# A long convolution and two expert layers on one core: the filter stage and the first two convolution chunks reordered

## The chip, the cores and the metric

The kernel runs on one core of a Trainium2 chip. The metric is device time in microseconds (us) of one execution; each kernel is run several times and the median counts. A profile is one execution, recorded apart from the timed runs.

## The reference, cut to what matters

```python
h_filt = (np.maximum(pos_emb @ w1, 0.0) @ w2) * np.exp(-0.01 * pos)[:, None]
u = x * v                                     # (2, 12480, 128)
y = irfft(rfft(u, 2 * S, axis=1) * rfft(h_filt, 2 * S, axis=0)[None], axis=1)[:, :S]
a = (x * y).reshape(24960, 128)
h = a @ moe_w_in;  b = where(h > 0, h, exp(min(h, 0)) - 1) @ moe_w_out     # 128 -> 2048 -> 128
h = b @ moe2_w_in; out = (h * cos(h)) @ moe2_w_out
```

A filter is made from position embeddings by two small matrix products, a long causal convolution is done through a Fourier transform, and two expert layers follow.

## The kernel before, in words

The program has three stages, each engine follows the written order of its own instructions (the schedule is written by hand), and TensorE (PE) runs through all of them.

**Filter** (lines 203 to 307). 16 chunks `c`. `rank(c)` (L257) is one product of the embeddings with `w1`; `relu(c)` (L262) takes it on ScalarE (ACT) to `r`, and GpSimd (POOL) splits `r` into a rounded part `r_h` and a rest `r_l`; `taps(c, half)` (L271) are 12 products a chunk with `w2`, and `window` (L280) scales them into `h_all` on VectorE (DVE) with one of eight columns left to ACT. `taps` follow `rank` three chunks behind. Products with a constant tile (`warm_up`, L216) fill PE before that.

**Convolution** (lines 310 to 477). 32 chunks of four channels, each with three sequences `k`: 0 and 1 are the two batches, 2 is the filter. For each, `st_a` (first transform, DVE's `za` and `zb`, POOL's `z_t`), `st_b` (second transform; for the filter ACT copies its result to `hr` and `hi_f`, for a batch DVE multiplies by them: `ya`, `ps_b`, `y_t`, and ACT rounds to `yh`), `lo_y` (POOL's rest `yl`), `st_c` (back transform, `wa`, `wb`, `w_t`) and `st_d` (last product, `at`, written to DRAM). `prod` (L318) makes `u_t` on POOL. A list `steps` (L465) gives one pass `p` its order; a step of the list works on chunk `p`, `p-1` or `p-2`. `ps_a`, `ps_b` and `ps_c` have one PSUM buffer each.

Between the steps the 64-bit weights of the expert layers are decoded, 32 jobs in two halves. `top` takes `Decode.bits` (L123) one piece further: piece 1 is `ps_w` and `sq` on ACT, piece 2 DVE's `size` and ACT's `keep`, piece 3 DVE's second `ps_w` and ACT's `power`, piece 4 DVE's `mag` and ACT's `lf`, then DVE's `pw` and piece 1 of the next job. `low` takes `Decode.parts` (L152) one piece further: POOL's product on `lf`; POOL's `full` (which reads `mag`) and ACT's `hi`; POOL's `lo` and the stores. A pass holds four `top` and three `low`. The tiles `mag`, `lf` and `pw` have two buffers, so those of job `j` take the place of those of job `j-2`.

**Expert layers** (lines 480 to 658), which the change doesn't touch.

```python
steps = ((st_b, 1, 0), (prod, 0, 1), (top, 0, 0), (lo_y, 1, 0), (low, 0, 0), (top, 0, 1), (st_a, 0, 2),
         (st_c, 2, 1), (top, 0, 2), (lo_z, 0, 2), (low, 0, 1), (st_b, 1, 1), (st_a, 0, 0), (lo_y, 1, 1),
         (st_d, 2, 0), (low, 0, 2), (st_c, 1, 0), (prod, -1, 0), (st_b, 0, 2), (st_a, 0, 1), (top, 0, 3),
         (st_d, 2, 1))
```

Of the kernel before, what the change touches and what calls it, by code (L numbers as in the profile page):

```python
# [9 lines left out]
F32 = mybir.dt.float32  # L10
# [3 lines left out]
AF = mybir.ActivationFunctionType  # L14
# [6 lines left out]
NB = 128  # L21
# [59 lines left out]
def hyena_moe_kernel(ctx: ExitStack, tc: tile.TileContext, x, v, pe, w1, w2,  # L81
# [92 lines left out]
    with tc.manual_schedule():  # L174
        nc.vector.memset(below, BELOW)
        with ExitStack() as cs:
# [26 lines left out]
            with ExitStack() as fs:  # L203
# [5 lines left out]
                ph = fs.enter_context(tc.tile_pool(name="ph", bufs=4, space=PSUM))  # L209
                NP = 4  # L210
                NCK = NB // 2 // NP
                NW = 3
                warm = f1.tile([128, 512], F32, name="warm")
                nc.vector.memset(warm, 0.5)

                def warm_up(n):  # L216
                    w_ps = pw.tile([128, 512], F32, name="w_ps")
                    nc.tensor.matmul(w_ps[:, 0:n], warm[:, 0:128], warm[:, 0:n], start=True, stop=True)  # L218

                w1_t = f1.tile([2 * FO, 2 * FO], F32, name="w1_t")  # L220
                w2_t = f1.tile([2 * FO, 2 * D], F32, name="w2_t")
                w2_h = f1.tile([2 * FO, 2 * D], F32R, name="w2_h")
# [6 lines left out]
                        nc.sync.dma_start(pes[c], pe[:, c * NP * NA:(c + 1) * NP * NA])  # L229

                load_pe(0)
                nc.vector.memset(w1_t, 0.0)
                nc.vector.memset(w2_t, 0.0)
                for k in range(2):
                    nc.scalar.dma_start(w1_t[k * FO:(k + 1) * FO, k * FO:(k + 1) * FO], w1)
                    nc.scalar.dma_start(w2_t[k * FO:(k + 1) * FO, k * D:(k + 1) * D], w2)
                nc.scalar.dma_start(win_t[:, :, 0], win)
                for c in range(1, 4):
                    load_pe(c)
                for _ in range(4):  # L240
                    warm_up(512)

                def load_tables():
                    nc.scalar.dma_start(fa_t, fa)
                    nc.scalar.dma_start(tw_t, tw)
                    nc.scalar.dma_start(ti_t, ti)
                    nc.scalar.dma_start(g_t, g)
                    nc.scalar.dma_start(dft_t, dft)

                def split_tables():  # L250
                    copy_r(dft_h, dft_t)
                    nc.vector.tensor_tensor(dft_l, dft_t, dft_h.bitcast(F32), op=ALU.subtract)

                copy_r(w2_h, w2_t)
                nc.vector.tensor_tensor(w2_l, w2_t, w2_h.bitcast(F32), op=ALU.subtract)
# [23 lines left out]

                def window(c, half):  # L280
                    ps, b = hp_.pop((c, half)), (2 * c + half) * NP
                    n = NP if half else NW
                    sl = slice(b, b + n)
                    nc.vector.tensor_tensor(h_all[:, :, sl].rearrange("a d b -> a b d"), ps[:, 0:n],
                                            win_t[:, sl].to_broadcast([NA, n, D]), op=ALU.mult)
                    for k in range(n, NP):
                        nc.scalar.activation(h_all[:, :, b + k], ps[:, k], AF.Copy, scale=win_t[:, b + k])

                for c in range(NCK + 4):
                    if c < NCK:  # L290
                        rank(c)
                        relu(c)
                    if 0 <= c - 3 < NCK:
                        taps(c - 3, 0)
                        taps(c - 3, 1)
                        window(c - 3, 0)
                        window(c - 3, 1)
                    if c < 3:
                        warm_up(512)
                        warm_up(512)  # L300
                    if c == 2:
                        load_tables()
                    if c == NCK - 2:
                        load(0)
                        load(1)
                    if c == NCK - 1:
                        split_tables()


            with ExitStack() as vs:  # L310
                p1 = vs.enter_context(tc.tile_pool(name="p1", bufs=1))
                p2 = vs.enter_context(tc.tile_pool(name="p2", bufs=2))
                pa = vs.enter_context(tc.tile_pool(name="pa", bufs=1, space=PSUM))
                pd = vs.enter_context(tc.tile_pool(name="pd", bufs=1, space=PSUM))
                bank = vs.enter_context(tc.tile_pool(name="bank", bufs=1, space=PSUM))
                us, zz, yy, hh, ww = {}, {}, {}, {}, {}

                def prod(c, k):  # L318
                    if c < NCH:
# [12 lines left out]
                    nc.gpsimd.tensor_tensor(yl, y, yh.bitcast(F32), op=ALU.subtract)  # L332
                    yy[c, k] = (yh, yl)

                def st_a(c, k):
                    ps = pa.tile([NB, 2, 512], F32, name="ps_a")
                    for s in range(DC):
                        lhs = h_all[:, c * DC + s] if k == 2 else us[c, k][:, s]
                        o = (s % 2) * 2 * NF
                        nc.tensor.matmul(ps[:, s // 2, o:o + 2 * NF], lhs, fa_t, start=True, stop=True)  # L340
                    n = 4 * NF
                    t1 = p2.tile([NB, 2 * n], F32, name="za")
                    t2 = p2.tile([NB, 2 * n], F32, name="zb")
                    for q, t in ((0, t1), (1, t2)):
                        nc.vector.tensor_tensor(bank2(t), ps[:, :, 0:n],  # L345
                                                tw_t[:, q:q + 1].to_broadcast([NB, 2, n]), op=ALU.mult)
                    z = p2.tile([NB, 2, DC * NF], F32, name="z_t")
                    nc.gpsimd.tensor_tensor(z.rearrange("p r (s k) -> p r s k", s=DC),  # L348
                                            parts(t1, NF), parts(t2, NF)[:, ::-1], op=ALU.add)
# [10 lines left out]
                    zz[c, k] = (zh, zl)  # L360

                def st_b(c, k):
                    ps = pa.tile([NB, 2, 512], F32, name="ps_b")
                    n = DC * NF
                    mS, C, Sn = (slice(q * NB, (q + 1) * NB) for q in range(3))
                    prs = (((C, 0), (Sn, 1)), ((C, 1), (mS, 0)))
                    z = zz.pop((c, k))
                    for r in range(2):
                        for j, (sl, q) in enumerate(prs[r]):
                            if k == 2:  # L370
                                zh, zl = z
                                mm = ((dft_h, zh), (dft_l, zh), (dft_h, zl))
                            else:
                                mm = ((dft_t, z),)
                            for i, (a, b) in enumerate(mm):
                                nc.tensor.matmul(ps[:, r, 0:n], a[:, sl], b[:, q], start=j == 0 and i == 0,  # L376
                                                 stop=j == 1 and i == len(mm) - 1)
# [19 lines left out]
                def st_c(c, k):  # L397
                    yh, yl = yy.pop((c, k))
                    last = c == NCH - 1
                    ps = pa.tile([NF, 2, 512], F32, name="ps_c", tag="ps_a" if last and k else "ps_c")  # L400
# [59 lines left out]
                def top(c, k):  # L460
                    next(bits, None)

                next(bits)
                prod(0, 0)
                steps = ((st_b, 1, 0), (prod, 0, 1), (top, 0, 0), (lo_y, 1, 0), (low, 0, 0), (top, 0, 1), (st_a, 0, 2),  # L465
                         (st_c, 2, 1), (top, 0, 2), (lo_z, 0, 2), (low, 0, 1), (st_b, 1, 1), (st_a, 0, 0), (lo_y, 1, 1),
                         (st_d, 2, 0), (low, 0, 2), (st_c, 1, 0), (prod, -1, 0), (st_b, 0, 2), (st_a, 0, 1), (top, 0, 3),
                         (st_d, 2, 1))
                for p in range(NCH + 2):
                    for f, back, k in steps:  # L470
                        if 0 <= p - back < NCH or f in (top, low):
                            f(p - back, k)
                    load(p + 2)
                for _ in bits:
                    pass
# [221 lines left out]
```

## Time and profile before

| | us |
|---|---|
| median of 3 runs (2925.21 to 2925.38) | 2925.26 |
| span of the profiled execution | 2922.3 |
| first taps of the filter | 17.30 |
| first `st_d` of the convolution | 90.06 |
| first product of the expert layers | 694.41 |

The span runs from the first to the last instruction; what lies around it is 3.0 us against the median of the runs. PE is busy 99% of the span, DVE 85%, ACT 73%, POOL 90%. [...] A timeline row that merges several instructions gives the start of the first and the time they cover.

### The profile page before, as it was taken

Reading aid. Unit: us, or ns where it says so; the run is one execution under the profiler, and the core shown is the slowest. Engines: PE = TensorE matmul, PEld = TensorE weight load, DVE = VectorE, ACT = ScalarE, POOL = GpSimd, SP = SyncE. Lnnn points to the kernel's source line nnn. Section 1 sums busy time; section 2 is a strip of 40 time slices with the busy share of each in tenths; the row PEclk is TensorE's granted clock in tenths of the full one; section 3 lists DMA queues with packets and bytes.
Section 4 is the critical chain, followed back from the end, with each engine's and each line's share of the span. In section 5 each row is a group of like instructions: output and inputs, shape, how many; then the busy total and the mean of one; then the engine's idle time right before and its main releaser. Section 6 shows DMA issues by size and latency. Waiting matters only on the chain.

```text
span 2922.3 us, 40341 instructions
## 1 busy us (share of the span) xinstructions
PE 2888.7 (99%) x13580; PEld 2393.3 (82%) x13580; DVE 2497.0 (85%) x3241; ACT 2146.6 (73%) x3332; POOL 2632.8 (90%) x1908
## 2 busy tenths in 40 slices
PE   8999999998999999999999999999999999999999
PEld 6878787886888888888888887888888888888887
DVE  5888888887998998899899998888888888888887
ACT  3322323224988898888888888888888888888887
POOL 4888888886999999999999998999999999999998
PEclk9999999998999999999999999999999999999999
DMA  3333333333000000000000001000000000000000
GB/s 105 90 81 88 97 89 86 88 83 97 14 11 14 11 12 14 14 11 11 14 11 14 11 11 60 11 14 11 14 11 14 11 11 14 11 14 11 13 12 14
DMA packets 83104, 96.82 MB, mean 33 GB/s; under 512 B 6106, under 2 KB 68088, under 8 KB 82898
## 3 DMA queue, kind: packets, MB, share of 16 engines
q1 hardware_dynamic: 77072, 88.20, 10.6%
q10 hardware_dynamic: 5826, 6.04, 0.7%
q8 instruction: 109, 1.79, 0.3%
q14 instruction: 97, 0.79, 0.1%
HBM read 59.94 MB, written 34.28 MB: 32 GB/s over the span
## 4 chain that ended last, share of the span: by engine, by line
PE 92%; ACT 3%; DVE 2%; issue 2%; POOL 1%; DMA 0%; ACTq 0%; POOLq 0%; DVEq 0%
PE h_ps L545 35%; PE o_ps L614 34%; PE ps_b L376 8%; PE ps_c L408 6%; PE ps_a L340 4%; PE ps_d L426 4%; ACT e L582 1%; DVE e L575 1%; DVE e L584 1%; ACT e L573 1%; PE h_ps L277 1%; ACT gh L97 1%; ACT ot L622 1%; PE w_ps L218 0%; PE r_ps L259 0%
## 5 line engine op out<-in xcount | busy, mean ns | idle before, releaser
L106 POOL TENSOR_TENSOR gl<-e,gh 128x960 fp32r<-128x960 f32 x780 | 1463.7, 1888 | 88.6 <-ACT gh L97 45.3
L545 PE MATMUL h_ps<-xh,w 128*128 128x480 f32 x3328 | 1022.3, 388 | 15.5 <-DVE e L562 5.5
L614 PE MATMUL o_ps<-gh,w 128*128 128x480 f32 x3120 | 933.0, 380 | 0.0
L545 PEld LDWEIGHTS h_ps<-xh,w 128*128 128x128 f32 x3328 | 623.0, 189 | 150.5 <-issue 26.6
L614 PEld LDWEIGHTS o_ps<-gh,w 128*128 128x128 f32 x3120 | 586.8, 188 | 92.9 <-POOL gh L105 0.2
L575 DVE SCALAR_TENSOR_TENSOR e<-e,h_ps 128x960 f32<-128x960 int32 x416 | 479.9, 1154 | 193.1 <-ACT e L573 67.0
L545 PE MATMUL h_ps<-xl,w 128*128 128x480 f32 x1664 | 634.6, 381 | 0.0
L560 DVE SCALAR_TENSOR_TENSOR e<-e,t_ps 128x480 f32<-128x480 f32 x832 | 539.6, 652 | 108.8 <-ACT t_ps L558 87.7
L614 PE MATMUL o_ps<-gl,w 128*128 128x480 f32 x1560 | 594.3, 381 | 2.0 <-POOL gl L106 2.0
L556 ACT ACTIVATE e<-h_ps 128x480 f32<-128x480 f32 x832 | 475.5, 572 | 141.6 <-PE h_ps L545 106.9
L573 ACT ACTIVATE e<-h_ps 128x960 int32<-128x960 f32 x416 | 404.1, 971 | 149.8 <-PE h_ps L545 148.0
L105 POOL TENSOR_SCALAR gh<-e 128x960 fp32r<-128x960 f32 x468 | 466.8, 998 | 42.1 <-DVE e L562 24.1
L558 ACT ACTIVATE t_ps<-h_ps 128x480 f32<-128x480 f32 x832 | 479.4, 576 | 0.0
L562 DVE SCALAR_TENSOR_TENSOR e<-e,h_ps 128x480 f32<-128x480 f32 x780 | 472.3, 647 | 0.0
L582 ACT ACTIVATE e<-e,half_pi 128x960 f32<-128x960 f32 x416 | 453.9, 1091 | 0.3 <-DVE e L575 0.3
L584 DVE TENSOR_TENSOR e<-e,h_ps 128x960 f32<-128x960 f32 x390 | 447.2, 1147 | 1.3 <-ACT e L582 1.2
L545 PEld LDWEIGHTS h_ps<-xl,w 128*128 128x128 f32 x1664 | 314.3, 189 | 52.3 <-POOL xl L106 0.6
L614 PEld LDWEIGHTS o_ps<-gl,w 128*128 128x128 f32 x1560 | 293.7, 188 | 50.6 <-POOL gl L106 3.2
L97 ACT ACTIVATE gh<-e 128x960 fp32r<-128x960 f32 x312 | 312.4, 1001 | 0.0
L376 PE MATMUL ps_b<-z_t,dft_t 128*128 128x360 f32 x512 | 165.7, 466 | 2.1 <-DVE y_t L392 1.7
L348 POOL TENSOR_TENSOR z_t<-za,zb 128x720 f32<-128x720 f32 x96 | 141.1, 1470 | 26.3 <-DVE zb L345 26.3
L408 PE MATMUL ps_c<-dft_h,yh 128*90 128x256 f32 x512 | 160.4, 313 | 0.0
(90 smaller groups left out, 3066.7 us busy)
## 6 DMA issues: line engine op xcount, KB each, us to landing
x_t<-in_x SPq DMA_DIRECT2D x32, 392.0 KB
v_t<-in_v SPq DMA_DIRECT2D x32, 392.0 KB
xt_d<-at SPq DMA_DIRECT2D x64, 196.0 KB
out<-ot SPq DMA_DIRECT2D x52, 240.0 KB
x_in<-xt_d SPq DMA_DIRECT2D x50, 240.0 KB
raw<-in_wi SPq DMA_DIRECT2D x16, 256.0 KB
w_d<-hi SPq DMA_DIRECT2D x32, 128.0 KB
w_d<-lo SPq DMA_DIRECT2D x32, 128.0 KB
```

What stands on the lines that cost most here:

```text
L105: ENG[plan[0]].tensor_scalar(hi, full, 1.0, 0.0, op0=ALU.mult, op1=ALU.add)
L106: ENG[plan[1]].tensor_tensor(lo, full, hi.bitcast(F32), op=ALU.subtract)
L545: nc.tensor.matmul(h[:, 0:T], a, b, start=k == 0, stop=k == 2)
L556: nc.scalar.activation(u[:, e], hs[e][:, 0:T], AF.Exp)
L558: nc.scalar.activation(ts[e][:, 0:T], hs[e][:, 0:T], AF.Tanh, scale=0.5)
L560: nc.vector.scalar_tensor_tensor(u[:, e], u[:, e], 1.0, ts[e][:, 0:T], op0=ALU.add, op1=ALU.mult)
L562: nc.vector.scalar_tensor_tensor(gt[:, e], u[:, e], 0.0, hs[e][:, 0:T], op0=ALU.min, op1=ALU.max)
L573: nc.scalar.activation(kq, hv, AF.Copy, scale=1.0 / TWO_PI, bias=0.25)
L575: nc.vector.scalar_tensor_tensor(rr, kq, -TWO_PI, hv, op0=ALU.mult, op1=ALU.add)
L582: nc.scalar.activation(rr, rr, AF.Sin, bias=half_pi)
L584: nc.vector.tensor_tensor(gt, rr, hv, op=ALU.mult)
L614: nc.tensor.matmul(o, a, b[:, e], start=f == 0 and k == 0, stop=f == NFT - 1 and k == len(mm) - 1)
```

## The change

In the filter, `taps` follow `rank` two chunks behind, and the first taps go ahead of the third rank; of ten warm-up products one is left. `w1` and `w2` are padded by the host to whole tiles and loaded by one transfer each, and the tables go over SyncE's queue. `window` splits its work evenly in the last two chunks, and `dft_l` moves from DVE to POOL. The pools of the convolution wait tile by tile for the memory that they take over. `st_b` is split into `mm_b` and `out_b`; the filter's products take all of `zh` ahead of `zl`. The first two passes are written out in another order with other PSUM buffers. Five `top` and one `low` lie in that part, where the list had eight and six; passes 8 to 11 each get one `top` more, behind `st_c(1, 0)`.

```diff
-                nc.vector.memset(w1_t, 0.0)
-                nc.vector.memset(w2_t, 0.0)
-                for k in range(2):
-                    nc.scalar.dma_start(w1_t[k * FO:(k + 1) * FO, k * FO:(k + 1) * FO], w1)
-                    nc.scalar.dma_start(w2_t[k * FO:(k + 1) * FO, k * D:(k + 1) * D], w2)
+                nc.scalar.dma_start(w1_t, w1)
+                nc.sync.dma_start(w2_t, w2)
...
-                for _ in range(4):
-                    warm_up(512)
+                nc.scalar.activation(cool, warm[:, 0:1], AF.Copy)
+                warm_up(512)
...
-                for c in range(NCK + 4):
-                    if c < NCK:
+                for c in range(NCK + 2):
+                    first = c == 2
+                    if c < NCK and not first:
                         rank(c)
                         relu(c)
-                    if 0 <= c - 3 < NCK:
-                        taps(c - 3, 0)
-                        taps(c - 3, 1)
-                        window(c - 3, 0)
-                        window(c - 3, 1)
-                    if c < 3:
-                        warm_up(512)
-                        warm_up(512)
+                    if c >= 2:
+                        taps(c - 2, 0)
+                        taps(c - 2, 1)
+                        window(c - 2, 0)
+                        window(c - 2, 1)
+                    if first:
+                        rank(c)
+                        relu(c)
...
-                    n = NP if half else NW
+                    n = (NP if half else NP - 1) if c < NCK - 2 else NP // 2
...
-                    nc.vector.tensor_tensor(dft_l, dft_t, dft_h.bitcast(F32), op=ALU.subtract)
+                    nc.gpsimd.tensor_tensor(dft_l, dft_t, dft_h.bitcast(F32), op=ALU.subtract)
...
-                p1 = vs.enter_context(tc.tile_pool(name="p1", bufs=1))
+                p1 = vs.enter_context(tc.tile_pool(name="p1", bufs=1, reuse_waits="tile"))
...
-                    z = p2.tile([NB, 2, DC * NF], F32, name="z_t")
+                    z = p2.tile([NB, 2, DC * NF], F32, name="z_t", bufs=3)
...
-                next(bits)
-                prod(0, 0)
...
-                for p in range(NCH + 2):
+                prod(0, 0)
+                prod(0, 1)
+                st_a(0, 0)
+                st_a(0, 2, "ps_b")
+                lo_z(0, 2)
+                st_a(0, 1, "ps_c")
+                prod(1, 0)
+                st_a(1, 2)
+                next(bits)
+                mm_b(0, 0)
+                mm_b(0, 2, "ps_c")
+                out_b(0, 2)
+                top(0, 0)
+                top(0, 0)
+                load(2)
+                out_b(0, 0)
+                lo_z(1, 2)
+                mm_b(0, 1, "ps_c")
+                out_b(0, 1)
+                lo_y(0, 0)
+                st_a(1, 0)
+                top(0, 0)
+                st_c(0, 0, "ps_b")
+                lo_y(0, 1)
+                prod(1, 1)
+                top(0, 0)
+                mm_b(1, 2, "ps_c")
+                out_b(1, 2)
+                st_a(1, 1)
+                prod(2, 0)
+                top(0, 0)
+                low(0, 0)
+                load(3)
+                for p in range(2, NCH + 2):
                     for f, back, k in steps:
                         if 0 <= p - back < NCH or f in (top, low):
                             f(p - back, k)
+                        if f is st_c and k == 0 and 8 <= p < 12:
+                            top(0, 0)
                     load(p + 2)
```

How the change moves instructions, at three places. First PE at the start of the program, before:

```order
L218 MATMUL w_ps<-warm 128x512 x4
L259 MATMUL r_ps<-pe_t,w_t 128x392
L218 MATMUL w_ps<-warm 128x512 x2
L259 MATMUL r_ps<-pe_t,w_t 128x392
L218 MATMUL w_ps<-warm 128x512 x2
L259 MATMUL r_ps<-pe_t,w_t 128x392
L218 MATMUL w_ps<-warm 128x512 x2
L259 MATMUL r_ps<-pe_t,w_t 128x392
L277 MATMUL h_ps<-w_h,r_h 98x256
```

and with the change:

```order
L217 MATMUL w_ps<-warm 128x512
L256 MATMUL r_ps<-pe_t,w_t 128x392 x2
L274 MATMUL h_ps<-w_h,r_h 98x256
L274 MATMUL h_ps<-w_l,r_h 98x256
L274 MATMUL h_ps<-w_h,r_l 98x256
```

The taps of the first chunk stand behind one warm-up and two ranks instead of ten warm-ups and four ranks.

Second, ACT behind the last windows, where the convolution begins, with the change (in brackets the engines and transfers that an instruction waits for):

```order
L284 ACTIVATE h_all<-h_ps,win_t 98x128
L97 ACTIVATE zh<-z_t 128x720 [waits DMAHW3_49,DMAHW4_49,DMAHW2_49,DMAHW7_49,DMAHW1_49,Pool_49]
L97 ACTIVATE zh<-z_t 128x720 [waits PE_49,Activation_49,Pool_49]
L136 ACTIVATE ps_w<-raw 128x256 [waits DMAHW4_49]
L137 ACTIVATE sq<-raw 128x256 [waits DMAHW5_49,DMAHW1_49,DMAHW0_49]
L388 ACTIVATE hr<-ps_b 128x360 [waits PE_49]
L389 ACTIVATE hi_f<-ps_b 128x360
L390 ACTIVATE hi_f<-ps_b 128x360
```

The `zh` of chunk 1 (the second row) stands ahead of `hr` and `hi_f` of chunk 0; before, only one `zh` stood there.

Third, DVE in a pass behind the twelfth, from `st_b(1, 0)` on, before:

```order
L389 TENSOR_TENSOR ya<-ps_b,hr 128x720 [waits DVE_49,PE_49,Activation_49]
L390 TENSOR_TENSOR ps_b<-ps_b,hi_f 128x2x360 [waits Activation_49]
L392 TENSOR_TENSOR y_t<-ya,ps_b 128x720 [waits DVE_49]
L139 TENSOR_SCALAR size<-ps_w 128x256 [waits Activation_49]
L143 SCALAR_TENSOR_TENSOR ps_w<-ps_w,size 128x256 [waits DVE_49]
L345 TENSOR_TENSOR za<-ps_a,tw_t 128x720 [waits PE_49,Pool_49]
L345 TENSOR_TENSOR zb<-ps_a,tw_t 128x720
L412 TENSOR_TENSOR wa<-ps_c,ti_t 90x1024 [waits PE_49,Pool_49]
L412 TENSOR_TENSOR wb<-ps_c,ti_t 90x1024
L147 SCALAR_TENSOR_TENSOR mag<-ps_w,keep 128x256 [waits DVE_49,Activation_49]
```

and with the change:

```order
L396 TENSOR_TENSOR ya<-ps_b,hr 128x720 [waits DVE_49,PE_49,Activation_49]
L397 TENSOR_TENSOR ps_b<-ps_b,hi_f 128x2x360 [waits Activation_49]
L399 TENSOR_TENSOR y_t<-ya,ps_b 128x720 [waits DVE_49]
L143 SCALAR_TENSOR_TENSOR ps_w<-ps_w,size 128x256
L147 SCALAR_TENSOR_TENSOR mag<-ps_w,keep 128x256 [waits DVE_49,Activation_49,Pool_49]
L343 TENSOR_TENSOR za<-ps_a,tw_t 128x720 [waits PE_49]
L343 TENSOR_TENSOR zb<-ps_a,tw_t 128x720
```

`mag` has moved up ahead of `za` and waits for POOL as well. On POOL, the piece of `low` behind the first `yl` of a pass was `lf` before:

```order
L332 TENSOR_TENSOR yl<-y_t,yh 128x720 [waits Activation_49]
L156 TENSOR_TENSOR lf<-lf,pw 128x256
```

and is `full` with the change:

```order
L330 TENSOR_TENSOR yl<-y_t,yh 128x720 [waits Activation_49]
L158 TENSOR_TENSOR full<-mag,lf 128x256 [waits Pool_49]
```

`low` has fallen two pieces behind, so that the `full` of job `p-2` stands in pass `p`, which is the pass in which `mag` of job `p` takes over its buffer.

## Rows read from the trace of the kernel before

**Rows 1.** Stretches: from:to, us, then PE, PEld, DVE, ACT, POOL busy, granted clock, DMA share, GB/s.

```profile
0.00:17.30 17.30, 15.47 (x28) 5.38 (x29) 1.38 (x5) 3.19 (x5) 4.40 (x10) 1.00 0.35 93
17.30:49.10 31.80, 31.29 (x218) 27.07 (x216) 27.13 (x31) 14.11 (x29) 18.21 (x26) 1.00 0.50 140
49.10:52.20 3.10, 1.25 (x9) 1.21 (x8) 1.72 (x3) 0.48 (x1) 2.14 (x2) 1.00 0.50 161
52.20:62.50 10.30, 6.49 (x22) 5.77 (x21) 4.53 (x7) 2.79 (x6) 5.06 (x4) 0.50 0.25 72
...
90.10:680.20 590.10, 590.02 (x3254) 471.44 (x3253) 519.52 (x660) 174.58 (x358) 492.96 (x390) 1.00 0.32 86
```

**Rows 2.** Timeline of the filter's start: start, us, engine, instruction, count, [idle before].

```profile
3.47 0.62 ACTq L236 DMA_DIRECT2D w_t<-in_w  x1
...
6.44 1.28 ACT L97 ACT_TABLE_LOAD   x1 [6.44 <-DMA win_t<-in_win]
...
8.85 0.82 PE L259 MATMUL r_ps<-pe_t,w_t 128*128 128x392 f32 x2
...
10.89 0.88 POOL L268 TENSOR_TENSOR r_l<-r,r_h 128x392 fp32r<-128x392 f32 x1
...
17.30 0.58 PE L277 MATMUL h_ps<-w_h,r_h 128*98 128x256 f32 x1
```

**Rows 3.** Timeline where filter and convolution meet, and PE at the first `st_d`.

```profile
48.84 0.28 PE L277 MATMUL h_ps<-w_h,r_l 128*98 128x256 f32 x1
...
69.78 2.66 PE L376 MATMUL ps_b<-z_t,dft_t 128*128 128x360 f32 x8 [1.70 <-DVE y_t L392]
...
90.06 1.88 PE L426 MATMUL ps_d<-w_t,g_t 90*98 90x512 f32 x4
```

**Rows 4.** Groups by line and form, 49.1 to 90.1 us: busy, mean ns, idle before.

```profile
L348 POOL TENSOR_TENSOR z_t<-za,zb 128x720 f32<-128x720 f32 x7 | 10.3, 1473 | 8.3 <-DVE zb L345 8.3
...
L321 POOL TENSOR_TENSOR u_t<-x_t,v_t 98x512 f32<-98x512 f32 x6 | 6.5, 1097 | 3.6 <-PE h_ps L277 3.6
...
L419 POOL TENSOR_TENSOR w_t<-wa,wb 90x1024 f32<-90x1024 f32 x2 | 4.0, 1998 | 0.4 <-DVE wb L412 0.4
...
L412 DVE TENSOR_TENSOR wa<-ps_c,ti_t 90x1024 f32<-90x1024 f32 x2 | 2.4, 1210 | 0.0
...
L97 ACT ACTIVATE zh<-z_t 128x720 fp32r<-128x720 f32 x3 | 2.4, 806 | 8.3 <-POOL z_t L348 8.3
```

**Rows 5.** Timeline of one pass in the steady part: PE, then DVE, POOL and ACT.

```profile
382.69 1.39 PE L340 MATMUL ps_a<-fa_t,u_t 98*128 98x180 f32 x8
...
402.27 1.39 PE L340 MATMUL ps_a<-fa_t,u_t 98*128 98x180 f32 x8
...
396.06 0.91 DVE L389 TENSOR_TENSOR ya<-ps_b,hr 128x720 f32<-128x720 f32 x1 [1.55 <-issue]
...
398.65 0.42 DVE L139 TENSOR_SCALAR size<-ps_w 128x256 int32<-128x256 int32 x1
...
399.44 0.90 DVE L345 TENSOR_TENSOR za<-ps_a,tw_t 128x720 f32<-128x720 f32 x1
400.25 0.90 DVE L345 TENSOR_TENSOR zb<-ps_a,tw_t 128x720 f32<-128x720 f32 x1
...
399.65 1.46 POOL L332 TENSOR_TENSOR yl<-y_t,yh 128x720 fp32r<-128x720 f32 x1 [2.19 <-ACT yh L97]
401.07 0.64 POOL L156 TENSOR_TENSOR lf<-lf,pw 128x256 f32<-128x256 f32 x1
...
393.95 0.42 ACT L136 ACTIVATE ps_w<-raw 128x256 f32<-128x256 f32 x1 [2.11 <-DVE pw L150]
...
398.76 0.81 ACT L97 ACTIVATE yh<-y_t 128x720 fp32r<-128x720 f32 x1 [4.04 <-DVE y_t L392]
```

**Rows 6.** Timeline of the way into the expert layers.

```profile
691.05 0.34 ACTq L523 DMA_DIRECT2D x_in<-xt_d  x1
...
693.76 0.59 POOL L105 TENSOR_SCALAR xh<-x_in 128x480 fp32r<-128x480 f32 x1 [4.77 <-DMA x_in<-xt_d]
```

More of the change, by code (lines that the diff above doesn't have):

```diff
@@ L211, in hyena_moe_kernel @@
                 NCK = NB // 2 // NP
-                NW = 3
                 warm = f1.tile([128, 512], F32, name="warm")
@@ L218, in warm_up @@
                     nc.tensor.matmul(w_ps[:, 0:n], warm[:, 0:128], warm[:, 0:n], start=True, stop=True)
+                cool = f1.tile([128, 1], F32, name="cool")
                 w1_t = f1.tile([2 * FO, 2 * FO], F32, name="w1_t")
@@ L239, in hyena_moe_kernel @@
                     load_pe(c)
-                for _ in range(4):
-                    warm_up(512)
+                nc.scalar.activation(cool, warm[:, 0:1], AF.Copy)
+                warm_up(512)
                 def load_tables():
[L244 to L248, printed above, removed]
+                    nc.sync.dma_start(fa_t, fa)
+                    nc.sync.dma_start(tw_t, tw)
+                    nc.sync.dma_start(dft_t, dft)
+                    nc.sync.dma_start(ti_t, ti)
+                    nc.sync.dma_start(g_t, g)
                 def split_tables():
                     copy_r(dft_h, dft_t)
-                    nc.vector.tensor_tensor(dft_l, dft_t, dft_h.bitcast(F32), op=ALU.subtract)
+                    nc.gpsimd.tensor_tensor(dft_l, dft_t, dft_h.bitcast(F32), op=ALU.subtract)
                 copy_r(w2_h, w2_t)
@@ L287, in window @@
                         nc.scalar.activation(h_all[:, :, b + k], ps[:, k], AF.Copy, scale=win_t[:, b + k])
-                for c in range(NCK + 4):
-                    if c < NCK:
+                for c in range(NCK + 2):
+                    first = c == 2
+                    if c < NCK and not first:
                         rank(c)
                         relu(c)
-                    if 0 <= c - 3 < NCK:
-                        taps(c - 3, 0)
-                        taps(c - 3, 1)
-                        window(c - 3, 0)
-                        window(c - 3, 1)
-                    if c < 3:
-                        warm_up(512)
-                        warm_up(512)
-                    if c == 2:
+                    if c >= 2:
[6 more added lines that the diff above has]
+                        relu(c)
+                    if c == 4:
@@ L302, in hyena_moe_kernel @@
                         load_tables()
-                    if c == NCK - 2:
+                    if c == NCK - 5:
                         load(0)
                         load(1)
-                    if c == NCK - 1:
+                    if c == NCK - 4:
                         split_tables()
             with ExitStack() as vs:
-                p1 = vs.enter_context(tc.tile_pool(name="p1", bufs=1))
-                p2 = vs.enter_context(tc.tile_pool(name="p2", bufs=2))
-                pa = vs.enter_context(tc.tile_pool(name="pa", bufs=1, space=PSUM))
@@ L314, in hyena_moe_kernel @@
-                pd = vs.enter_context(tc.tile_pool(name="pd", bufs=1, space=PSUM))
-                bank = vs.enter_context(tc.tile_pool(name="bank", bufs=1, space=PSUM))
-                us, zz, yy, hh, ww = {}, {}, {}, {}, {}
+                p1 = vs.enter_context(tc.tile_pool(name="p1", bufs=1, reuse_waits="tile"))
+                p2 = vs.enter_context(tc.tile_pool(name="p2", bufs=2, reuse_waits="tile"))
+                pa = vs.enter_context(tc.tile_pool(name="pa", bufs=1, space=PSUM, reuse_waits="tile"))
@@ L318, in prod @@
+                pd = vs.enter_context(tc.tile_pool(name="pd", bufs=1, space=PSUM, reuse_waits="tile"))
+                bank = vs.enter_context(tc.tile_pool(name="bank", bufs=1, space=PSUM, reuse_waits="tile"))
+                us, zz, bb, yy, hh, ww = {}, {}, {}, {}, {}, {}
                 def prod(c, k):
@@ L333, in lo_y, with st_a @@
                     yy[c, k] = (yh, yl)
-                def st_a(c, k):
-                    ps = pa.tile([NB, 2, 512], F32, name="ps_a")
+                def st_a(c, k, tag="ps_a"):
+                    ps = pa.tile([NB, 2, 512], F32, name="ps_a", tag=tag)
                     for s in range(DC):
@@ L362, in st_b, with mm_b @@
                 def st_b(c, k):
-                    ps = pa.tile([NB, 2, 512], F32, name="ps_b")
+                    mm_b(c, k)
+                    out_b(c, k)
+                def mm_b(c, k, tag="ps_b"):
+                    ps = pa.tile([NB, 2, 512], F32, name="ps_b", tag=tag)
                     n = DC * NF
@@ L367, in st_b, with out_b @@
                     z = zz.pop((c, k))
[L368 to L377, printed above, removed]
+                    if k == 2:
+                        zh, zl = z
+                        mm = (((dft_h, zh), (dft_l, zh)), ((dft_h, zl),))
+                    else:
+                        mm = (((dft_t, z),),)
+                    for g, part in enumerate(mm):
+                        for r in range(2):
+                            for j, (sl, q) in enumerate(prs[r]):
+                                for i, (a, b) in enumerate(part):
+                                    nc.tensor.matmul(ps[:, r, 0:n], a[:, sl], b[:, q], start=g + j + i == 0,
+                                                     stop=g == len(mm) - 1 and j == 1 and i == len(part) - 1)
+                    bb[c, k] = ps
+                def out_b(c, k):
+                    ps, n = bb.pop((c, k)), DC * NF
                     if k == 2:
@@ L395, in st_b, with st_c @@
                     yy[c, k] = (y, yh)
-                def st_c(c, k):
+                def st_c(c, k, tag="ps_c"):
                     yh, yl = yy.pop((c, k))
                     last = c == NCH - 1
-                    ps = pa.tile([NF, 2, 512], F32, name="ps_c", tag="ps_a" if last and k else "ps_c")
+                    ps = pa.tile([NF, 2, 512], F32, name="ps_c", tag="ps_a" if last and k else tag)
                     n = 2 * NB
@@ L673, in seq, with pair @@
         return np.ascontiguousarray(p.reshape(B, NA, NB, D).transpose(1, 0, 3, 2))
+    def pair(a):
+        a = np.asarray(a)
+        n, m = a.shape
+        p = np.zeros((2 * n, 2 * m), a.dtype)
+        p[:n, :m] = p[n:, m:] = a
+        return p
     def words(a):
@@ L684 @@
         pe=np.ascontiguousarray(pp.reshape(NA, NB // 2, 2, FO).transpose(2, 3, 1, 0)).reshape(2 * FO, NB // 2 * NA),
-        w1=np.ascontiguousarray(inputs["w1"]), w2=np.ascontiguousarray(inputs["w2"]),
+        w1=pair(inputs["w1"]), w2=pair(inputs["w2"]),
         wi1=words(inputs["moe_w_in"]), wo1=words(inputs["moe_w_out"]),
```

## The prediction, made before the changed kernel had run

> **What bounds the kernel now.** I read the stretches first. From the first `st_d` to the end of the convolution, PE is busy 590.02 of 590.10 us at full clock (last of [rows 1]): only time on PE counts there, and the other engines must hand over in time. [...] The first taps start at 17.30 [rows 2], though they need only two small weights and one chunk of `r`. [...] Next I read one steady pass on the timeline: `st_a(0, 0)` starts at 382.69 and again at 402.27, so a pass is 19.58 us [rows 5]. The slack of the hand-overs in that pass decides this change.
>
> **The filter's start.** The last of four loads of `w1` and `w2` was issued until 3.47 + 0.62 = 4.09, and a load issued behind it on the same queue was used at 6.44, 2.35 after that [rows 2] (`w_t` there stands for both weights). `w1` is now the first and only load of that queue, issued by about 1.4; it lands near 3.8. The warm-ups that stood in the way on PE are gone but for one. From a rank's start to the end of its `r_l` it takes 8.85 to 11.77, 2.92 us; I add 0.6 because PE has then hardly worked. The first taps start near 7.4 instead of 17.30: −9.9. Two more ranks now lie inside the stretch of the taps (14, not 12), at most 0.82 each: +1.6. The stretch was full on PE but for 0.5 us (31.29 of 31.80 [rows 1]), which may go: −0.5. Last tap near 40.3: **about −9**. The other loads (tables on SyncE, `x_t`, `v_t` issued three ranks earlier) have 10 us and more before their use, and the DMA share was 0.50 [rows 1]: counted at nothing, at most 2 us if they slip.
>
> **From the last tap to the first `st_d`.** "Tile by tile" does not help the first step: `u_t(0, 0)` on POOL still waits for the last tap, as before (the 3.6 us of idle time before `u_t` [rows 4]). Counting from the last tap: `u_t` 1.1, then three `st_a`, each followed by `za` and `zb`, 0.81 apart, so `z_t(0, 2)` ends near +7.6, `zh` near +8.5, `zl` near +10.0, and PE has done `mm_b(0, 0)` and `mm_b(0, 2)` by +10.7. The next product, `mm_b(0, 1)`, takes over the PSUM buffer that `hi_f` reads. `hi_f` stands on ACT behind `zh` of chunk 1, which waits for POOL's `z_t(0, 1)`, `u_t(1, 0)` and `z_t(1, 2)`: 1.45 + 1.1 + 1.45 behind `zl`, +14.0. Then `zh` 0.8, and `ps_w`, `sq`, `hr` and two `hi_f`, five copies of about 0.4 (the 0.42 of `ps_w`, [rows 5]): +16.7. PE stands **6.0 us** still. Later `st_a(1, 1)` waits for `u_t(1, 1)`, which stands on POOL behind `w_t` and `yl`: `wa` and `wb` 2.4, `w_t` 2.0, `yl` 1.46, `u_t` 1.1 [rows 4, 5] are 7.0 us, of which `mm_b(1, 2)` covers 2: **5 us** more. In sum: the pause ends at +16.7; four groups of products (`mm_b(0, 1)` to `mm_b(1, 2)`) fill 9.0 us, the second pause 5.3, and six groups (`st_a(1, 1)` to `st_a(2, 0)`) 11.3 us, as in a full pass of 19.58 us, which holds three `st_a`, three `st_b`, two `st_c` and two `st_d`. The first `st_d` comes 42.3 us behind the last tap instead of 41.0: +1.3 at full clock.
>
> What does the clock do there? In [rows 1] it fell to 0.50 right behind a stretch in which PE worked 1.25 of 3.10 us, and stayed for 10.30 us with 6.49 us of work, some 3.2 us lost. A pause of 1.70 us at 69.78 [rows 3] was followed by no fall. Two pauses of 5 to 6 us are longer than both. I take one such loss for each and take off what before lost: 2 × 3.2 − 3.2 = 3.2, and 0.8 for slower starts, **+4**; ends 0 (no fall) and +10 (low clock through the whole stretch, whose products take some 25 us, less the loss of before, at a share of it). [...]
>
> Both terms together: −9 + 1.3 + 4 = **−4** (ends −8 and +2; the first if no clock falls, the second if the low clock goes on).
>
> **The steady passes.** This is the term that decides. `low` was at work six times in the first two passes, and is now once; `top` got four more pieces in passes 8 to 11. From pass 12 on `bits` is a piece ahead and `low` two behind. DVE's `mag` of job `p` takes the buffer of job `p-2`, so it waits for POOL's `full` of job `p-2`, and that stands in the same pass, right behind `yl`. `yl` in turn comes from DVE's own `ya`, `ps_b`, `y_t` of this pass. From [rows 5]: `ya` starts 396.06; `y_t` ends about 398.7; ACT's `yh` 398.76 to 399.57; POOL's `yl` 399.65 to 401.11; `full`, as long as the `lf` in that place, 401.07 to 401.71. `mag` can start at about 401.77, and takes 0.41 as `size` does. `za` stands behind it and starts at 402.1, not at 399.44: 2.67 late. DVE does work in its order: `ps_w` was ready at 394.37, yet `size` waited for `ya` and its two followers until 398.65 while DVE had been idle 1.55 us before `ya`. So `zb`, which ended at 401.15, ends near 403.83, and PE's `st_a(0, 0)`, which has to wait for it (one `ps_a`), starts near 403.9 instead of 402.27: 1.12 us of the delay is slack, **1.6 us is new idle time of PE**. From there to the next `st_b(1, 0)` PE has no other wait, so the loop closes at 21.2 us a pass, and nothing makes up for it. The passes 12 to 31 are 20, each with a job to decode: 20 × 1.6 = 32, and half a microsecond for a weaker wait in the first ones: **+32.5**. The hand-overs of 0.02 to 0.1 us between engines, five in that chain, make it 1.3 to 1.9 a pass: +26 to +38. Ends: nothing, and 20 × 2.67 = 53 if the slack of 1.12 is used up otherwise.
>
> **The way into the expert layers.** ACT's last `hi` comes later, so the last weight stores and the loads behind them are issued just ahead of `x_in`; this was issued until 691.39 and used at 693.76 [rows 6]. **+1**, ends 0 and +3. The expert layers keep their order: 0.
>
> **Sum.** −4 + 32.5 + 1 = +29.5. The profiled span of 2922.3 becomes 2951.8, and with the 3.0 us around it (median 2925.26) the time is **2955 us**.
>
> **The rivals.**
> 1. *The wait on `full` is hidden: faster.* If `full` of job `p-2` is done before DVE gets to `mag` (it needs to be 1.6 us earlier than I have it, which it is if `low` is one piece further ahead than I count, in front of `yl`), only the start counts: −4 + 1 and a little, 2922; with full clock 2917. For it: POOL is idle 2.19 us before `yl` [rows 5], time enough for a `full` of 0.64 placed there. Against: in the new order it stands behind `yl`, and POOL takes its work in order. 0.10.
> 2. *Half of the passes.* The wait binds in only ten passes, because the backlog of `low` is caught up: +16 instead of +32.5, 2938. Each pass still holds three `low` for one job, so nothing catches up. 0.04.
> 3. *The clock falls in every pass.* A pause of 1.6 us in each of 20 passes could bring the low clock each time; at 3.2 us lost for one fall [rows 1], +64 more, near 3020. Against: the pause of 1.70 us at 69.78 left the stretch around it at full clock. 0.05. [...]
> 4. *The change doesn't do what it says:* the waits by tile free nothing early, which my count already has for `u_t`; were `u_t` free at its data, the sum would fall by 1 to 2. Inside the range.
>
> **How the numbers follow.** Forecast 0.80, the rivals 0.10, 0.04, 0.05, and 0.01 for nothing visible. The forecast's ends: −8 + 26 + 0 = +18 and +2 + 38 + 3 = +43, each with all terms at one end; 2943 to 2968. All at the upper end is unlikely, so 2965; the lower end I put at 2941 for a part of the second rival. A measurement of this kernel can tell about 0.2%, 5.9 us. Faster: the first rival, 0.10. Same: 0.02, between. Slower: 0.88.
>
> **What would show it.** Right: first taps near 7.4; first `st_d` near 86; pauses of about 6 and 5 us behind the third and sixth group of the convolution; from pass 12 a pass of about 21.2 us, DVE idle before `mag` with POOL's `full` as releaser, PE idle before `st_a(0, 0)` with DVE's `zb` as releaser; expert layers as long as before. Wrong: a steady pass still at 19.6 us, or a `full` that ends before DVE gets to `mag`.

## The result, and the profile after

The changed kernel takes **2960.03 us** (median of 4 runs, 2958.44 to 2960.98), the kernel before 2925.32 (4 runs): 1.0116 times as long, with a 95% interval of 1.0104 to 1.0129. The forecast was 2955, 2941 to 2965. The profiled execution spans 2959.2 us against 2922.3, 36.9 longer. That is 2.2 more than the medians differ; the profiled execution was the slowest of the four, 0.95 us above their median.

The stretches, with the columns of [rows 1], cut where the new kernel's stages meet (last tap at 39.55, first `st_d` at 87.43):

```profile
0.00:6.64 6.64, 4.76 (x6) 1.50 (x6) 0.97 (x3) 2.40 (x4) 0.73 (x5) 1.00 0.59 163
6.64:39.55 32.91, 32.91 (x222) 28.02 (x220) 26.61 (x31) 15.78 (x35) 22.82 (x32) 1.00 0.67 183
39.55:49.50 9.95, 8.67 (x47) 7.59 (x48) 7.25 (x9) 2.20 (x6) 6.36 (x5) 1.00 0.14 42
49.50:56.20 6.70, 1.17 (x7) 0.72 (x5) 1.44 (x3) 2.60 (x7) 5.53 (x5) 0.93 0.00 0
56.20:67.90 11.70, 11.61 (x52) 9.24 (x52) 8.38 (x11) 2.67 (x5) 2.94 (x2) 0.75 0.11 27
67.90:72.90 5.00, 0.00 (x0) 0.00 (x0) 0.77 (x2) 2.23 (x6) 4.46 (x3) 0.95 0.22 72
72.90:87.43 14.53, 14.50 (x64) 11.80 (x65) 9.26 (x12) 2.12 (x5) 7.63 (x7) 0.78 0.10 29
87.43:263.59 176.16, 176.16 (x974) 140.95 (x973) 156.66 (x203) 53.14 (x113) 148.22 (x117) 1.00 0.33 92
263.59:372.11 108.52, 100.92 (x542) 78.56 (x541) 85.76 (x111) 29.07 (x61) 82.39 (x65) 0.98 0.31 84
372.11:670.55 298.44, 277.23 (x1514) 218.00 (x1513) 240.92 (x309) 81.67 (x168) 231.08 (x183) 1.00 0.30 82
```

The filter is over 9.6 us earlier than in [rows 1, 3]. Then come two stretches in which PE hardly works, 49.50 to 56.20 and 67.90 to 72.90, and behind each one a mean clock of 0.75 and 0.78. Up to 263.59 the passes are full. From then on they are not: 277.23 of 298.44 us in the last row, at full clock.

A mean clock between the levels mixes two stretches, one at 1.00, full speed, and one at 0.50. Cut where the clock changes, the stretches that the rows give at 0.50 up to 372 us are these three:

```profile
55.31:62.13 6.82, 5.86 (x12) 3.79 (x13) 3.53 (x5) 2.43 (x6) 2.09 (x2) 0.50 0.00 0
72.37:79.20 6.83, 6.27 (x15) 4.70 (x16) 2.05 (x3) 0.00 (x0) 2.03 (x3) 0.50 0.22 61
328.37:331.79 3.42, 3.42 (x10) 1.73 (x9) 3.39 (x6) 1.30 (x4) 3.01 (x2) 0.50 0.02 5
```

The first two begin inside the pauses, 0.96 and 0.56 us before their ends at 56.27 and 72.93, and reach into the work behind them. The third lies among the steady passes: PE had stood for 1.51 us until 326.52, had then worked at full clock (1.00 up to 328.37), and was at work throughout the stretch.

What PE waited for over the whole run (total us, times, longest):

```profile
PE ps_a L338 <- DVE zb L343: 30.3, 20, 1.5
PE h_ps L585 <- POOL xh L105: 7.4, 1, 7.4
PE ps_a L338 <- POOL u_t L319: 6.3, 2, 5.0
PE ps_b L379 <- ACT hi_f L390: 5.6, 1, 5.6
```

And DVE's waits between 264 and 690 us:

```profile
DVE mag L147 <- POOL full L158: 53.3, 20, 2.7
```

One pass shows how the two belong together. The timeline of DVE, POOL, ACT and PE in a pass that answers to [rows 5]:

```profile
512.16 0.91 DVE L396 TENSOR_TENSOR ya<-ps_b,hr 128x720 f32<-128x720 f32 x1 [1.38 <-issue]
...
513.93 0.91 DVE L399 TENSOR_TENSOR y_t<-ya,ps_b 128x720 f32<-128x720 f32 x1
...
514.86 0.81 ACT L97 ACTIVATE yh<-y_t 128x720 fp32r<-128x720 f32 x1 [6.54 <-DVE y_t L399]
...
515.75 1.46 POOL L330 TENSOR_TENSOR yl<-y_t,yh 128x720 fp32r<-128x720 f32 x1 [1.27 <-ACT yh L97]
...
517.17 0.64 POOL L158 TENSOR_TENSOR full<-mag,lf 128x256 f32<-128x256 f32 x1
...
517.84 0.42 DVE L147 SCALAR_TENSOR_TENSOR mag<-ps_w,keep 128x256 int32<-128x256 int32 x1 [2.67 <-POOL full L158]
...
518.18 0.90 DVE L343 TENSOR_TENSOR za<-ps_a,tw_t 128x720 f32<-128x720 f32 x1
519.00 0.90 DVE L343 TENSOR_TENSOR zb<-ps_a,tw_t 128x720 f32<-128x720 f32 x1
...
520.04 1.46 PE L338 MATMUL ps_a<-fa_t,u_t 98*128 98x180 f32 x8 [1.52 <-DVE zb L343]
```

DVE sits idle for 2.67 us before `mag`, `za` and `zb` follow late, and PE starts `st_a(0, 0)` 7.88 us behind `ya` instead of 6.21 (402.27 − 396.06 in [rows 5]). That is 1.67; the eight products are 0.07 slower behind the pause (1.46 against 1.39), and a pass takes 21.32 us instead of 19.59: **+1.73**.

The way into the expert layers, which answers to [rows 6]:

```profile
718.82 0.42 ACT L97 ACTIVATE hi<-full 128x256 fp32r<-128x256 f32 x1 [5.67 <-POOL full L158]
718.83 5.71 ACTq L548 DMA_DIRECT2D w<-w_d  x8
...
722.78 2.25 PE L433 MATMUL ps_d<-w_t,g_t 90*98 90x512 f32 x4 [2.46 <-POOL w_t L423]
...
728.88 0.34 ACTq L563 DMA_DIRECT2D x_in<-xt_d  x1
...
732.41 1.17 PE L585 MATMUL h_ps<-xh,w 128*128 128x480 f32 x2 [7.38 <-POOL xh L105]
```

The balance, from the starts of the `st_d` groups and of the first expert product:

| from, to | before, us | after, us | difference |
|---|---|---|---|
| start, first `st_d` | 90.06 | 87.43 | −2.6 |
| first to last `st_d` | 598.98 | 635.35 | +36.4 |
| last `st_d` to the first expert product | 5.37 | 9.63 | +4.3 |
| from there to the end of the span | 2227.9 | 2226.8 | −1.1 |

Of the 36.4, 20 passes by 1.73 are 34.6. The rest is mainly one pass of 22.97 us instead of 21.32, the one with the clock at 0.50 from 328.37 to 331.79 (a `st_d` group there took 3.06 us instead of 1.88).

### The profile page after: what moved, and what is told of

It is laid out like the page before. It is cut to its first block, busy times and chain, and to the rows that moved or that the text cites. A ratio compares the mean times of both kernels' runs of the same rounds, so it can differ in the third digit from the quotient of the medians.

```text
span 2959.2 us, 40211 instructions
## 1 busy us (share of the span) xinstructions
PE 2888.3 (98%) x13562; PEld 2390.5 (81%) x13562; DVE 2493.2 (84%) x3238; ACT 2146.6 (73%) x3339; POOL 2636.4 (89%) x1909
## 4 chain that ended last, share of the span: by engine, by line
PE 84%; DVE 6%; ACT 3%; issue 3%; POOL 3%; DMA 1%; POOLq 0%; ACTq 0%; SPq 0%; DVEq 0%
PE h_ps L585 35%; PE o_ps L654 34%; PE ps_b L379 4%; PE ps_c L415 4%; PE ps_d L433 3%; PE ps_a L338 3%; POOL yl L330 1%; DVE e L615 1%; ACT e L622 1%; DVE e L624 1%; PE h_ps L274 1%; ACT e L613 1%; DVE za L343 1%; DVE zb L343 1%; DVE ya L396 1%
## 5 line engine op out<-in xcount | busy, mean ns | idle before, releaser
L97 ACT ACTIVATE yh<-y_t 128x720 fp32r<-128x720 f32 x64 | 51.8, 809 | 270.8 <-DVE y_t L399 270.8
```

## The experiments

The theory: in twenty passes DVE's `mag` waits for POOL's `full`, and that alone makes them longer. The rivals: the passes are longer for something else in the new convolution code; the start is worth nothing, or all it promised. Each kernel was compared with the kernel before on the same chip.

**e1_mag3: a third buffer.**

```diff
-                    return pool.tile([128, 256], dt, name=name, tag=f"d_{name}")
+                    return pool.tile([128, 256], dt, name=name, tag=f"d_{name}", bufs=3 if name == "mag" else None)
```

> The changed kernel, with a third buffer for `mag` and nothing else. Theory (the stall in passes 12 to 31 is `mag` waiting for `full` of two jobs before, in its own buffer): the wait is gone, a pass is 19.6 us again instead of 21.32, 21 passes by 1.73 = 36.4 us less: 2960.0 - 36.4 = 2923.6 us. Rival (the passes are longer for another reason: the tile-wise waits, the third buffer of `z_t`, or four pieces more of decoding): still 2950 to 2960 us.

Measured: 2924.1 us, 0.9995 (0.9986 to 1.0004) of before. Passes of 19.57 us but for one of 19.87, and no wait of PE for `zb` any more. The order of every engine is the changed kernel's; only the buffer differs. So the stall is this wait, at the size of the whole difference in the passes.

**e3_notops: the order alone.** Without the four `top` in passes 8 to 11.

```diff
-                        if f is st_c and k == 0 and 8 <= p < 12:
-                            top(0, 0)
```

> The changed kernel without the four additional `top` of passes 8 to 11. Theory: `mag` of a job comes four pieces later and finds `full` done; passes of 19.6 us: 2921 to 2926 us. Rival (the first two passes alone put `low` too far behind): the stall stays, 2950 to 2960 us.

Measured: 2922.5 us, 0.9991 (0.9982 to 1.0000). All passes 19.57 us. The two buffers are enough as long as `mag` doesn't come too early.

**e2_onelow: the other half brought nearer by one piece.**

```diff
                             top(0, 0)
+                            if p == 8:
+                                low(0, 0)
```

> The changed kernel with one piece of `low` more, in pass 8 behind its additional `top`; buffers as they are. Theory (it is the distance between the two halves of the decoding): `full` of job p-2 is done a pass earlier, in front of `mag`; passes of 19.6 us, and the last stores of weights come a little earlier, which takes 0 to 3 us off the way into the expert layers: 2920 to 2924 us. Rival (buffer or engine time is short whatever the distance): 2945 us and more.

Measured: 2938.1 us, 1.0046 (1.0031 to 1.0061), a miss. The wait for `zb` was gone, but the passes were 20.05 us. What PE waited for in this kernel:

```profile
PE ps_b L379 <- ACT hi_f L390: 14.0, 23, 5.6
```

ACT, POOL and PE in one of its passes:

```profile
497.57 0.64 POOL L158 TENSOR_TENSOR full<-mag,lf 128x256 f32<-128x256 f32 x1
...
498.24 0.42 ACT L97 ACTIVATE hi<-full 128x256 fp32r<-128x256 f32 x1 [4.39 <-POOL full L158]
498.57 0.45 ACT L388 ACTIVATE hr<-ps_b 128x360 f32<-128x360 f32 x1
498.92 0.46 ACT L389 ACTIVATE hi_f<-ps_b 128x360 f32<-128x360 f32 x1
499.27 0.47 ACT L390 ACTIVATE hi_f<-ps_b 128x360 f32<-128x360 f32 x1
...
499.88 2.66 PE L379 MATMUL ps_b<-z_t,dft_t 128*128 128x360 f32 x8 [0.24 <-ACT hi_f L390]
```

The additional piece moved `full` from behind the first `yl` of a pass to behind the second. There ACT's copy `hi`, which waits for `full`, stands ahead of `hr` and `hi_f`, on which PE's next `st_b` waits. One wait went, another came, a quarter of its size. The theory was right on `mag` and silent on this place.

**e5_twolow: two pieces.**

```diff
                             top(0, 0)
+                            if p < 10:
+                                low(0, 0)
```

> The changed kernel with two pieces of `low` more (passes 8 and 9), the additional `top` kept. With one more, the wait of `mag` was gone but PE waited 0.4 us a pass for `hi_f`, because `full` and ACT's `hi` had come into the place ahead of `hr` and `hi_f`. Theory (each place in the pass allows only some pieces; two more bring `low` back to the places of the kernel before): passes of 19.6 us behind the tenth, no wait for `mag` nor for `hi_f`, some 3 us for the two passes that hold more: 2921 to 2927 us. Rival (any further piece costs in every pass): 2935 us and more.

Measured: 2925.7 us, 1.0000 (0.9991 to 1.0009). Passes of 19.57 us from the tenth on, with one of 19.86; the two passes that hold the additional pieces took 24.27 and 19.91 together with them. In the first of these PE stood 2.8 us for `hi_f`, and from 216.75 to 220.16 the clock was 0.50, so not all of its 4.7 us is the pieces' own. Not the number of pieces counts, but the place at which each falls.

**g_before_far: the stall in the kernel before.** Its own filter, chunks and buffers; only the two halves of the decoding are set apart.

```diff
+                        if f is low and p < 2 and (p, k) != (1, 2):
+                            continue
                         if 0 <= p - back < NCH or f in (top, low):
                             f(p - back, k)
+                        if f is st_c and k == 0 and p == 8:
+                            top(0, 0)
```

> The kernel before, its filter, its first chunks and its buffers as they were, but with one `low` instead of six in the first two passes and one `top` more, in pass 8. Theory (the stall is nothing but the distance between the two halves of the decoding): passes of 21.3 us from pass 9 or 10 on, PE waiting for DVE's `zb` in each: 2925 + 22 x 1.73 = 2963 us, 2955 to 2968. Rival (the stall needs the tile-wise waits or another part of the new code): 2925 to 2930 us.

Measured: 2968.5 us, 1.0148 (1.0132 to 1.0163); passes of 21.33 us from pass 9 on. What PE waited for:

```profile
PE ps_a L340 <- DVE zb L345: 37.9, 24, 3.4
PE h_ps L549 <- POOL xh L105: 8.5, 1, 8.5
```

Of the 24 waits for `zb`, the one of 3.4 us stands in the first chunk, where before had it too; 23 belong to the passes. The old kernel gets the same pass length, and a long wait for `xh` at the end, from nothing but that distance. None of the 23 pauses brought the clock down: from 73.07 us to the last `st_d` it is 1.00.

**e4_filter: the new filter in the kernel before.** The section from the weights' loads to the tables' split, taken over whole.

```diff
-                for c in range(NCK + 4):
+                for c in range(NCK + 2):
...
-                for _ in range(4):
-                    warm_up(512)
+                warm_up(512)
```

> The kernel before with the new filter stage alone (loads of the weights, one warm-up, order of ranks and taps, window); the convolution as before. Theory (the filter's part is worth what its last tap shows, 39.55 instead of 49.12): first `st_d` near 80.5, passes of 19.6 us, 2925.3 - 9.6 = 2915.8 us. Rival (the start is given back behind it, by a lower clock or by x_t and v_t coming late): 2920 to 2925 us.

Measured: 2918.8 us, 0.9976 (0.9968 to 0.9985): 6.2 us less, not 9.6. The last tap comes at 40.93, the first `st_d` at 83.38, which is 42.5 us later and not 40.9. Before, one stretch at 0.50 follows the last tap (52.25 to 62.49). Here there are two:

```profile
44.69:54.93 10.24, 7.15 (x23) 6.70 (x24) 4.48 (x7) 2.88 (x7) 5.43 (x4) 0.50 0.31 88
61.76:65.17 3.41, 3.41 (x7) 1.96 (x6) 2.40 (x4) 1.20 (x3) 2.95 (x3) 0.50 0.01 2
```

The second one is new. It takes in most of the eight products that stand behind PE's pause of 1.70 us for `y_t`:

```profile
61.45 4.35 PE L374 MATMUL ps_b<-z_t,dft_t 128*128 128x360 f32 x8 [1.70 <-DVE y_t L390]
```

In [rows 3] the same products stand behind the same pause and take 2.66 us. The difference, 1.69, is about what was given back behind the last tap (42.5 instead of 40.9). So the filter alone is a gain: 8.2 us at this kernel's last tap, 6.7 at its first `st_d`, 6.2 between the medians.

**f3_fill: the two pauses filled.** On e3, five products on constant tables stand in each pause; nothing reads them.

```diff
+                fill(5)
                 mm_b(0, 1, "ps_c")
...
+                fill(5)
                 st_a(1, 1)
```

> The changed kernel without the four additional `top` (2922.5 us), orders as they are, but with five products on constant tables in each of the two pauses (before `mm_b(0, 1)` and before `st_a(1, 1)`); their result is not used. Theory (the pauses bring the clock down, and that costs about 5.6 us besides the pauses themselves): the granted clock stays 1.00, first `st_d` some 42.5 us behind the last tap instead of 47.9: 2917 to 2918 us. Rival (the low clock has another cause, or costs nothing on the path): 2922 to 2924 us.

Measured: 2918.0 us, 0.9977 (0.9969 to 0.9986), against 2922.5 and 0.9991 (0.9982 to 1.0000) for e3. From the last tap (40.15) to the first `st_d` it takes 42.3 us:

```profile
50.00:56.20 6.20, 5.55 (x17) 2.43 (x16) 0.84 (x3) 2.00 (x5) 5.29 (x5) 1.00 0.00 0
56.20:82.47 26.27, 24.64 (x127) 18.75 (x127) 19.00 (x26) 7.62 (x18) 15.37 (x13) 1.00 0.15 41
```

The pauses in the work are as long as they were; the clock stays at 1.00. The intervals of f3 and e3 overlap a little, but the profiles agree with the medians: from the last tap to the first `st_d` e3 takes 46.4 us, 4.1 more than f3. So the low clock of these two places came from PE's standing still. It cost 4.1 us in e3's profile and 47.9 − 42.3 = 5.6 us in the changed kernel's, with the same code. What differs is where the stretches at 0.50 lie. In e3 they begin earlier in the pauses, and less of PE's work falls into them, 3.65 and 4.72 us instead of 5.86 and 6.27:

```profile
52.99:59.82 6.83, 3.65 (x6) 2.17 (x7) 3.39 (x5) 4.13 (x9) 2.76 (x3) 0.50 0.00 0
70.06:76.88 6.82, 4.72 (x12) 3.92 (x13) 1.85 (x3) 0.09 (x1) 2.04 (x2) 0.50 0.20 59
```

Half of that work is 4.2 us in e3 and 6.1 in the changed kernel, near the 4.1 and 5.6 measured.

**f1_zh: ACT's order.** On e3, `zh` of chunk 1 behind `hr` and `hi_f` of chunk 0.

```diff
-                        copy_r(zh, z)
+                        if c != 1:
+                            copy_r(zh, z)
                         z = (z, zh)
...
                 out_b(0, 2)
+                copy_r(zz[1, 2][1], zz[1, 2][0])
```

> The changed kernel without the four additional `top` (2922.5 us) and with ACT's `zh` of chunk 1 written behind `hr` and `hi_f` of chunk 0. Theory (the pause of 5.6 us before `mm_b(0, 1)` is ACT's order): that pause shrinks to about 1 us, part of it comes back later at `u_t(1, 1)`, first `st_d` 3 us earlier, and the clock falls less: 2916 to 2920 us. Rival (POOL's chain decides, whatever ACT's order): within 1 us of 2922.5.

Measured: 2919.5 us, 0.9979 (0.9970 to 0.9988), 3 us less than e3, whose interval it overlaps. The wait for `hi_f` fell from 5.6 to 1.4 us, that of 5.0 us for `u_t` stayed; first `st_d` at 81.68 instead of 85.90.

**f2_zh_u: and POOL's order.** As f1, with `prod(1, 1)` ahead of `lo_y(0, 0)`.

```diff
                 out_b(0, 1)
+                prod(1, 1)
                 lo_y(0, 0)
...
                 lo_y(0, 1)
-                prod(1, 1)
```

> As f1, and POOL's `u_t(1, 1)` written ahead of `yl(0, 0)`, so that it doesn't stand behind `w_t` and the second `yl`. Theory (both pauses are one engine's order, and the low clock follows from them): first `st_d` 7.5 us earlier than with neither, and up to 5 us more from the clock: 2910 to 2915 us. Rival (a third wait takes their place): 2916 to 2920 us.

Measured: **2913.1 us**, 0.9960 (0.9947 to 0.9972), faster than both kernels. From the last tap at 39.38 to the first `st_d` at 74.30 it is 34.9 us, at full clock throughout:

```profile
39.38:74.30 34.92, 30.16 (x168) 25.45 (x169) 27.18 (x35) 11.61 (x27) 26.52 (x21) 1.00 0.16 43
```

So the first two chunks in the new order are worth 6.0 us against the 40.9 of before, once two instructions stand elsewhere.

**h1_tail: the way into the expert layers.** On f2, two pieces for each `low` of the last two passes.

```diff
                             f(p - back, k)
+                        if f is low and p >= NCH:
+                            low(0, 0)
```

> As f2, and in the last two passes of the convolution each `low` takes two pieces, so that the last `hi` and `lo` are done earlier. Theory (the way into the expert layers is 4.3 us longer because the last `hi` on ACT comes late, the eight weight loads behind it are issued in one burst, and `x_in` can't be issued before the first of them has landed): PE's wait for `xh` falls from 7.5 to about 3 us, of which 1 us goes to POOL's other order: 2913.1 - 3 = 2910 us. Rival (the weights' transfers take their time wherever they begin): within 1 us of 2913.

Measured: 2911.8 us, 0.9951 (0.9939 to 0.9964). Its interval overlaps that of f2, so the time is inconclusive. The wait itself did what the theory said:

```profile
PE h_ps L587 <- POOL xh L105: 3.2, 1, 3.2
```

From the last `st_d` to the first expert product it is 6.4 us instead of 9.6. One late pass took 10.16 instead of 9.11, with PE waiting 0.8 us for POOL's `yl`: a third of the gain was given back by the pieces put in. The first expert product came only 0.5 us earlier (681.86 instead of 682.39), because the first `st_d` was already 1.5 us later (75.85 instead of 74.30), ahead of anything that the edit touches: in this profile the clock was 0.50 from 58.20 to 61.61, around the end of a pause of 2.0 us for `yl` that f2's profile has too, there at full clock. In e5 the wait for `xh` was 3.1 us as well. That `x_in` waits for one of the eight loads is argued from their order in the program and from the times, not shown by itself: `x_in` was issued 10.1 us behind the start of these loads in the changed kernel and in e3, 10.9 in g. The last store of `at` is not what it waits for: before, `x_in` was issued at 691.05 and that `at` was made at 691.37.

## Why the prediction was right

The forecast came out 5 us low, inside its range, and 7.4 low in the profiled span (2951.8 for 2959.2). The passes (3.9) and the tail (3.3) were the larger part of that. The steady passes, which it called the term that decides, were right in mechanism and near in size. In the first two chunks the mechanism was right, and the closeness of the number is in part luck. The tail was outside its ends.

*The filter's start: −9, measured −9.6 at the last tap* (39.55 against 49.12). First taps at 6.64, not 7.4: the first product takes `r_h` and `w_h` alone, and `r_l`, to whose end the forecast counted, is used two products later. The 0.6 added for the first products was due: the two products of a rank took 1.68 us there against 0.82 in [rows 2], though the row of that stretch gives the clock as 1.00. In before it was the same with the warm-ups: the first eight products took 7.52 us, the next four 2.20.

*First two chunks: +1.3 and +4, measured +6.9* (47.88 against 40.94). Both pauses are where they were said to be and as long: 5.6 us for 6.0, with `hi_f` as releaser, and 5.05 for 5.3 with `u_t`. At full clock the distance is 42.3, as worked out; f3 has it to the tenth. The clock did fall at both pauses. It cost 5.6 us, where +4 was put down, inside the ends of 0 and +10. But the working of the +4 was wrong. It took off the 3.2 us that before had lost, although the 41.0 us of before (from 48.84 + 0.28 to 90.06 in [rows 3]), against which the +1.3 is counted, already hold them; two falls at its price are +6.4. And a fall cost less than 3.2: five profiles with this same start (this kernel, e1, e2, e3, e5) have 46.3 to 48.0 us from the last tap to the first `st_d`, that is 4.0 to 5.7 us for the two falls together, by how much of the low clock fell into the pauses. The two errors work against each other. The 0.8 put down for slower starts no run shows: at full clock the eight products behind a pause took 1.46 us against 1.39, and in before 2.66 against 2.58. The trace gives 0.50 from the last 0.96 and 0.56 us of the two pauses into the work behind them, up to 62.13 and 79.20, and then 1.00; in f3, where the pauses are filled, it gives 1.00 throughout.

*Both together: −4, measured −2.6.*

*The steady passes: +32.5, measured +36.4.* The step that decided was right in each of its links: `mag` released by `full`, 2.67 us of idle time on DVE (20 times, 53.3 in total), 20 waits of PE for `zb`, no other wait in the pass. From `ya` to PE's start it was worked out as 7.84 us; it was 7.88. The forecast rounded 1.63 to 1.6 and left out that the products behind a pause take longer (1.46 us against 1.39); by 1.73 the twenty passes are 34.6, inside 26 to 38. Most of the rest, 1.65 us, is the one fall of the clock near 328 us, which the sum did not have.

*The tail: +1 with ends 0 and +3, measured +4.3.* Outside its ends. The step "this was issued until 691.39 and used at 693.76" counted only how late `x_in` would land; it took no account that `x_in` itself could be issued later. The last `hi`, at 718.82, stands ahead of eight loads on ACT's queue, and `x_in`, behind them, is issued 6.1 us after the last `st_d`'s start instead of 2.0. From the first expert product to the end, put at 0, it is 1.1 us less; the reason stays open.

*The rivals.* The hidden wait (2922) is what e1 and e3 make of it, with a buffer or without the early pieces; in the changed kernel nothing hid it. The stall in half of the passes didn't come. The clock fall in each pass came in one of twenty (0.50 from 328.37 to 331.79); the other nineteen pauses of 1.5 us had none, nor had the 23 in g. The argument put against this rival, that no fall followed the pause of 1.70 us at 69.78, held for that one execution: in e4, and in g, the same pause was followed by one, and the eight products behind it took 4.35 us instead of 2.66.

## What to carry to other kernels

Where a pipeline's two halves share tiles with two buffers, the distance between them is part of the schedule: count in which step the reader of job `p-2` runs, and what stands in front of it on its engine, before a filler piece is moved anywhere. A filler that waits for another engine stalls all that is written behind it, so it costs whatever of its wait the slack behind it doesn't take up, even where the engines have idle time to spare: here 1.67 of 2.67 us, besides the 0.07 us by which the products behind the pause were slower. And a shorter start was worth its gain here only as far as PE kept working behind it: of the 9.6 us at the last tap 2.6 were left at the first `st_d`.

## What the runs showed of the hardware that was not expected

Two pauses of 5 to 6 us were each followed by a stretch at 0.50, and that cost 4.0 to 5.7 us besides the pauses, from one profile to another of the same code. The price was near half of the PE work that fell into the low stretches (12.1 us of it in the changed kernel, 8.4 in e3). Products of no use in these pauses kept the clock at 1.00 and earned 4.1 us between the profiles of e3 and f3, 4.5 between the medians.

Pauses of 1.5 to 2.0 us did not decide by their length whether the clock fell. Of twenty of 1.5 us one was followed by 0.50, of 23 in g none. The pause of 1.70 us in the old first chunks was followed by 1.00 in before and by 0.50 in e4 and g; one of 2.0 us went with 1.00 in f2 and with 0.50 in h1. Such a fall cost 1.65 us near 328 us and 1.69 us in e4. What decides it, no run here shows.
